# K^T through fp32 words that hold two bf16 values: half as many TensorE transposes in a cached attention decode kernel

## The chip, the cores and the metric

The kernel runs on one core of one Trainium2 chip. The metric is the device time in microseconds (us) of one execution. One chunk below is 2048 cache rows of one head: 1 MB of K and 1 MB of V; there are 256 chunks.

## The reference, cut to what matters

```python
x = A_x                                             # (1, 1, 448)
q = (x @ wq).reshape(1, 1, 16, 256)                 # 16 query heads, 8 KV heads
k = jnp.repeat(k_cache, 2, axis=1)                  # k_cache, v_cache: (1, 8, 65536, 256) bf16
v = jnp.repeat(v_cache, 2, axis=1)
scores = jnp.einsum("bhqd,bhkd->bhqk", q, k) * (256 ** -0.5)
a = jnp.einsum("bhqk,bhkd->bhqd", softmax(scores), v) @ wo     # reshapes cut
# b: a small token-mixing MLP of x, g: a sigmoid gate;  out = g * a + (1 - g) * b
```

The two caches are 537 MB, read once. Everything else is small.

## The kernel before

K and V go through a ring of five 4 MB buffers, one load each for four chunks. TensorE (PE) needs K^T as stationary data for the scores, so every 128x128 block of K is transposed through PSUM. VectorE and ScalarE copy the transposes back to SBUF. Two cuts are marked.

```python
ring = sb([P, NS, DC * NT, DH], bf16, "ring")       # NS = 5 buffers, DC = 4 chunks, NT = 16 tiles, DH = 256
ktT  = sb([P, KTB, NB, 1024], bf16, "ktT")
kst  = psum([P, NB, 1024], bf16, "kst")             # NB = 4 banks
# ... cut ...
def transposes(c):
    # ... waits for the load and for the copies out of kst cut ...
        for j in range(8):
            ntl, dh = divmod(j, 2)
            ins = pe.transpose(kst[:, b, j * P:(j + 1) * P],
                               ring[:, slot, ck * NT + 4 * b + ntl, dh * P:(dh + 1) * P], ident[:, :])
        ins.then_inc(sem_tr, 1)
def scores(c):
    for nt in range(NT):
        b, ntl = divmod(nt, 4)
        for dh in range(2):
            j = 2 * ntl + dh
            ins = pe.matmul(sps[:, c % 2, 2 * nt:2 * nt + 2], ktT[:, slot, b, j * P:(j + 1) * P],
                            qT[:, dh, REP * g:REP * g + REP], start=(dh == 0), stop=(dh == 1))
def values(c):                                       # V is stationary, read with a stride of 2
    # for each of 16 tiles, for dj in 0, 1:
        ins = pe.matmul(acc[:, g % 2, col:col + REP], ring[:, slot, n, dj:DH:2], pT[:, c % PTB, 2 * nt:2 * nt + 2], ...)
for s in range(NC + LAG):                            # NC = 256 chunks
    transposes(s); scores(s - 1); denominators(s - 2); values(s - 2)   # the last 8 chunks' values come at the end
```

Per chunk PE issues 32 transposes, 32 scores matmuls, 1 denominator, 32 values matmuls, each as a weight load and a matmul.

The softmax here doesn't subtract the row's maximum and nothing guards it: scores larger than these inputs give would overflow.

## Time and profile before

| | before |
|---|---|
| time, median of 3 (range) | 1320.84 us (1320.27 to 1323.95) |
| profiled execution | 1318.47 us, span 1316.7 us |
| PE busy, mean granted clock | 86%, 0.765 |
| HBM traffic | 544 MB |

Lines of the page of the kernel before: busy time by engine, granted clock and DMA by slice in tenths, two DMA queues (packets, MB, share of 16 engines' span), and three groups of instructions (count, busy us, mean ns, idle before them).

```profile
PE 1125.9 (86%) x25054; PEld 1098.6 (83%) x25054; DVE 413.8 (31%) x716; ACT 549.1 (42%) x786; POOL 0.9 (0%) x7
...
PEclk9788877787886878777677686677677686887878
DMA  9999999999999999999999999999999999999992
...
q1 hardware_dynamic: 21330, 544.22, 97.1%
q8 instruction: 197, 3.23, 1.0%
...
L261 PE MATMUL kst<-ident,ring 128*128 128x128 bf16 x8192 | 701.3, 263 | 64.3 <-issue 33.0
...
L277 PEld LDWEIGHTS sps<-qT,ktT 128*128 128x128 bf16 x8192 | 248.7, 100 | 53.3 <-issue 52.5
L305 PEld LDWEIGHTS acc<-pT,ring 128*128 128x128 bf16 x8192 | 231.9, 99 | 61.2 <-issue 61.0
```

The DMA row is full but for the tail: the kernel is bound by its data stream. PE is nearly as full, at a clock that moves between full and half. The queue named "instruction" is 197 packets of 16 KB, which are 197 x 256 instructions of 64 bytes, as many as PE executes (2 x 25054 and a few hundred waits). The Trainium skill, "Runtime: NRT & Kernel Launch", section "Instruction fetch mechanics", describes this: an engine's instruction memory is a FIFO that is refilled by DMA in blocks of 16 KiB or 256 instructions. It calls the cost "mostly hidden".

The end of the kernel before: the values of the last eight chunks, then the last projection.

```profile
1304.39 6.04 PE L305 MATMUL acc<-pT,ring 128*128 128x2 bf16 x222
...
1310.88 1.07 PE L305 MATMUL acc<-pT,ring 128*128 128x2 bf16 x34 [0.45 <-issue]
...
1312.70 1.65 PE L317 MATMUL acc<-wo_sb,oTn 128*1 128x448 bf16 x4 [0.76 <-DVE oTn L465]
```

### The profile page before, as it was taken

Reading aid. Unit: us, or ns where it says so; the run is one execution under the profiler, and the core shown is the slowest. Engines: PE = TensorE matmul, PEld = TensorE weight load, DVE = VectorE, ACT = ScalarE, POOL = GpSimd, SP = SyncE. Lnnn points to the kernel's source line nnn. Section 1 sums busy time; section 2 is a strip of 40 time slices with the busy share of each in tenths; the row PEclk is TensorE's granted clock in tenths of the full one; section 3 lists DMA queues with packets and bytes.
Section 4 is the critical chain, followed back from the end, with each engine's and each line's share of the span. In section 5 each row is a group of like instructions: output and inputs, shape, how many; then the busy total and the mean of one; then the engine's idle time right before and its main releaser. Section 6 shows DMA issues by size and latency. Waiting matters only on the chain.

```text
span 1316.7 us, 53063 instructions
## 1 busy us (share of the span) xinstructions
PE 1125.9 (86%) x25054; PEld 1098.6 (83%) x25054; DVE 413.8 (31%) x716; ACT 549.1 (42%) x786; POOL 0.9 (0%) x7
## 2 busy tenths in 40 slices
PE   4888788888889878888888989898888988888887
PEld 4878788888889878888888988888888888888887
DVE  3686232222232322222222222232223232232222
ACT  2444444444444434344334434344444343443433
POOL 0000000000000000000000000000000000000000
PEclk9788877787886878777677686677677686887878
DMA  9999999999999999999999999999999999999992
GB/s 403 430 422 429 430 427 428 424 431 430 430 428 427 426 429 426 426 423 427 424 407 429 429 427 409 418 413 433 426 404 433 414 427 428 426 425 426 418 419 116
DMA packets 21559, 547.62 MB, mean 416 GB/s; under 512 B 2264, under 2 KB 4315, under 8 KB 4702
## 3 DMA queue, kind: packets, MB, share of 16 engines
q1 hardware_dynamic: 21330, 544.22, 97.1%
q8 instruction: 197, 3.23, 1.0%
q14 instruction: 20, 0.16, 0.0%
q10 hardware_dynamic: 12, 0.01, 0.0%
HBM read 544.22 MB, written 0.00 MB: 413 GB/s over the span
## 4 chain that ended last, share of the span: by engine, by line
PE 60%; DMA 31%; issue 8%; DVE 0%; ACT 0%; ACTq 0%; DVEq 0%
PE kst L261 36%; DMA ring<-in_A_k_cache_dram 30%; PE acc L305 11%; PE sps L277 11%; DMA b_b<-in_B_b_dram 1%; PE acc L288 1%; PE acc L317 1%; PE acc L325 0%; PE sps L356 0%; DVE ktT L488 0%; ACT L529 0%; PE sps L358 0%; DVE out_b L479 0%; DVE stat L409 0%; ACTq L521 0%
## 5 line engine op out<-in xcount | busy, mean ns | idle before, releaser
L551 ACT ACTIVATE ktT<-kst 128x1024 bf16<-128x1024 bf16 x512 | 512.0, 1022 | 690.8 <-PE kst L261 690.5
L261 PE MATMUL kst<-ident,ring 128*128 128x128 bf16 x8192 | 701.3, 263 | 64.3 <-issue 33.0
L261 PEld LDWEIGHTS kst<-ident,ring 128*128 128x128 bf16 x8192 | 647.3, 122 | 79.4 <-issue 45.2
L488 DVE COPY ktT<-kst 128x1024 bf16<-128x1024 bf16 x512 | 352.5, 691 | 857.8 <-PE kst L261 844.6
L305 PE MATMUL acc<-pT,ring 128*128 128x2 bf16 x8192 | 252.0, 164 | 56.6 <-issue 56.3
L277 PE MATMUL sps<-qT,ktT 128*128 128x2 bf16 x8192 | 255.5, 164 | 49.7 <-issue 49.3
L277 PEld LDWEIGHTS sps<-qT,ktT 128*128 128x128 bf16 x8192 | 248.7, 100 | 53.3 <-issue 52.5
L305 PEld LDWEIGHTS acc<-pT,ring 128*128 128x128 bf16 x8192 | 231.9, 99 | 61.2 <-issue 61.0
L542 ACT ACTIVATE pT<-sps 128x32 bf16<-128x32 f32 x256 | 50.3, 197 | 48.1 <-PE sps L277 48.0
L288 PE MATMUL acc<-pT,ones_sq 128*128 128x32 bf16 x256 | 45.9, 179 | 0.5 <-ACT pT L542 0.3
L288 PEld LDWEIGHTS acc<-pT,ones_sq 128*128 128x128 bf16 x256 | 25.1, 98 | 0.4 <-ACT pT L542 0.4
L340 PE MATMUL acc<-ones_sq,ktT 1*128 1x1 bf16 x28 | 0.9, 161 | 13.3 <-DMA b_b<-in_B_b_dram 13.3
L340 PEld LDWEIGHTS acc<-ones_sq,ktT 1*128 1x128 bf16 x28 | 0.8, 99 | 13.4 <-DMA b_b<-in_B_b_dram 13.4
L317 PE MATMUL acc<-wo_sb,oTn 128*1 128x448 bf16 x32 | 10.5, 467 | 0.8 <-DVE oTn L465 0.8
L536 ACT ACTIVATE zring<-zring 128x448 bf16<-128x448 bf16 x14 | 8.1, 580 | 0.3 <-issue 0.2
L441 DVE TENSOR_TENSOR zring<-wtmp,uring 128x448 bf16<-128x448 bf16 x14 | 5.5, 392 | 1.5 <-issue 0.5
L439 DVE TENSOR_TENSOR wtmp<-uring 128x448 bf16<-128x448 bf16 x14 | 5.5, 392 | 1.2 <-issue 0.2
L459 DVE TENSOR_TENSOR gu<-wtmp,zring 128x448 bf16<-128x448 bf16 x14 | 5.5, 392 | 1.0
L325 PE MATMUL acc<-gu,w2p_b 128*1 128x448 bf16 x14 | 5.8, 415 | 0.0
L445 DVE TENSOR_TENSOR zring<-uring,wtmp 128x448 bf16<-128x448 bf16 x14 | 5.5, 392 | 1.0
L528 ACT ACTIVATE statb<-statb 1x1 bf16<-1x1 bf16 x1 | 0.2, 206 | 13.2 <-DVE statb L411 13.2
L317 PEld LDWEIGHTS acc<-wo_sb,oTn 128*1 128x1 bf16 x32 | 2.4, 93 | 3.7 <-issue 1.7
(66 smaller groups left out, 63.3 us busy)
## 6 DMA issues: line engine op xcount, KB each, us to landing
ring<-in_A_k_cache_dram SPq DMA_DIRECT2D x64, 4096.0 KB, 29.8
ring<-in_A_v_cache_dram SPq DMA_DIRECT2D x63, 4096.0 KB, 32.3
wo_sb<-in_A_wo_dram SPq DMA_DIRECT2D x8, 448.0 KB, 29.4
ring<-in_A_wq_dram SPq DMA_DIRECT2D x1, 3072.0 KB, 19.3
ring<-in_A_v_cache_dram SPq DMA_DIRECT2D x1, 2048.0 KB, 30.5
ring<-in_A_v_cache_dram SPq DMA_DIRECT2D x1, 1024.0 KB, 32.6
ring<-in_A_v_cache_dram SPq DMA_DIRECT2D x2, 512.0 KB, 33.7
ring<-in_A_wq_dram SPq DMA_DIRECT2D x1, 512.0 KB, 20.1
```

Source lines behind the costliest of these rows:

```text
L261: ins = pe.transpose(kst[:, b, j * P:(j + 1) * P], ring[:, slot, ck * NT + 4 * b + ntl, dh * P:(dh + 1) * P], ident[:, :])
L277: ins = pe.matmul(sps[:, c % 2, 2 * nt:2 * nt + 2], ktT[:, slot, b, j * P:(j + 1) * P], qT[:, dh, REP * g:REP * g + REP], start=(dh == 0), ...
L288: pe.matmul(acc[:, g % 2, DENC:DENC + 2 * NT], ones_sq[:, :], pT[:, c % PTB, :], start=(k == 0), stop=(k == NCPH - 1))
L305: ins = pe.matmul(acc[:, g % 2, col:col + REP], ring[:, slot, n, dj:DH:2], pT[:, c % PTB, 2 * nt:2 * nt + 2], start=False, stop=(k == NCPH ...
L317: ins = pe.matmul(acc[0:1, g % 2, PRC:PRC + DM], oTn[:, g % 2, dj * REP + hh:dj * REP + hh + 1], wo_sb[:, g % 2, hh, dj * DM:(dj + 1) * DM ...
L325: pe.matmul(acc[0:1, 1, PRC:PRC + DM], w2p_b[:, kt:kt + 1], gu[:, kt % NUR, :], start=(kt == 0), stop=(kt == FT - 1)).then_inc(s_bmm, 1)
L439: vec.tensor_tensor(W, U, U, op=ALU.mult)
L441: vec.tensor_tensor(Z, W, U, op=ALU.mult)
L488: vec.tensor_copy(ktT[:, c % KTB, b, :], kst[:, b, :]).then_inc(sem_evd, 1)
L536: act.activation(zring[:, slot, :], zring[:, slot, :], AF.Tanh).then_inc(s_tanh, 1)
L542: act.activation(pT[:, c % PTB, :], sps[:, c % 2, 0:2 * NT], AF.Exp, scale=scale).then_inc(sem_exp, 1)
L551: act.activation(ktT[:, c % KTB, b, :], kst[:, b, :], AF.Copy).then_inc(sem_eva, 1)
```

## The change

The same bytes of K are read as fp32 words, each holding two neighbouring bf16 values, and transposed as such: 16 transposes per chunk instead of 32. The intent is to halve the costliest group on PE. In K^T even and odd columns of the head then alternate, so the scores matmul reads it with a stride of 2, and q is built in even and odd halves to match. The diff, cut to its core:

```diff
+        ring_f = ring.bitcast(f32)
-        ident = sb([P, P], bf16, "ident")
+        ident = sb([P, P], f32, "ident")
-        kst = psum([P, NB, 1024], bf16, "kst")
+        kst = psum([P, NB, 512], f32, "kst")
+        kst_b = kst.bitcast(bf16)
-                    for j in range(8):
-                        ntl, dh = divmod(j, 2)
+                    for j in range(4):
                         ins = pe.transpose(kst[:, b, j * P:(j + 1) * P],
-                                           ring[:, slot, ck * NT + 4 * b + ntl, dh * P:(dh + 1) * P],
-                                           ident[:, :])
+                                           ring_f[:, slot, ck * NT + 4 * b + j, :], ident[:, :])
@@ scores
-                                        ktT[:, slot, b, j * P:(j + 1) * P],
-                                        qT[:, dh, REP * g:REP * g + REP],
+                                        ktT[:, slot, b, ntl * DH + dj:(ntl + 1) * DH:2],
+                                        qT[:, dj, REP * g:REP * g + REP],
@@ cut: the q projection takes every second column of wq; the copies read kst_b, same bytes
```

More of the change, by code (lines that the diff above doesn't have):

```diff
@@ L274, in scores @@
                     b, ntl = divmod(nt, 4)
-                    for dh in range(2):
-                        j = 2 * ntl + dh
+                    for dj in range(2):
                         ins = pe.matmul(sps[:, c % 2, 2 * nt:2 * nt + 2],
-                                        ktT[:, slot, b, j * P:(j + 1) * P],
-                                        qT[:, dh, REP * g:REP * g + REP],
-                                        start=(dh == 0), stop=(dh == 1))
+                                        ktT[:, slot, b, ntl * DH + dj:(ntl + 1) * DH:2],
+                                        qT[:, dj, REP * g:REP * g + REP],
+                                        start=(dj == 0), stop=(dj == 1))
                 ins.then_inc(sem_qk, 1)
@@ L349, in _ @@
                     pe.wait_ge(sem_wq, 32)
-                    for dh in range(2):
+                    for dj in range(2):
                         for h in range(HQ):
-                            j = dh * HQ + h
-                            col = h * DH + dh * P
+                            j = dj * HQ + h
+                            col = h * DH
                             a, cb = divmod(col, HALF)
                             for kt in range(WF):
-                                pe.matmul(sps[:, 1, j:j + 1], wq_a[:, kt, col:col + P], xcol[:, kt:kt + 1],
-                                          start=(kt == 0), stop=False)
-                            ins = pe.matmul(sps[:, 1, j:j + 1], wq_b[:, cb:cb + P],
+                                pe.matmul(sps[:, 1, j:j + 1], wq_a[:, kt, col + dj:col + DH:2],
+                                          xcol[:, kt:kt + 1], start=(kt == 0), stop=False)
+                            ins = pe.matmul(sps[:, 1, j:j + 1], wq_b[:, cb + dj:cb + DH:2],
                                             xcol[:, WF + a:WF + a + 1], start=False, stop=True)
@@ L487, in _ @@
                         vec.wait_ge(sem_tr, NB * c + b + 1)
-                        vec.tensor_copy(ktT[:, c % KTB, b, :], kst[:, b, :]).then_inc(sem_evd, 1)
+                        vec.tensor_copy(ktT[:, c % KTB, b, :], kst_b[:, b, :]).then_inc(sem_evd, 1)
                 if c == 1:
@@ L550, in _ @@
                         act.wait_ge(sem_tr, NB * c + b + 1)
-                        act.activation(ktT[:, c % KTB, b, :], kst[:, b, :], AF.Copy).then_inc(sem_eva, 1)
+                        act.activation(ktT[:, c % KTB, b, :], kst_b[:, b, :], AF.Copy).then_inc(sem_eva, 1)
                 if c >= 1:
```

## The prediction

> **What bounds the kernel now.** The DMA queue. The table of slices shows the 16 DMA engines at 9 tenths in 39 of 40 slices; the stretches from 50 to 1250 us show a DMA share of 1.00 at 420 to 428 GB/s. The queue table gives 544 MB, busy 97.1% of 1316.7 us. The issue list has 30 to 32 us from issue to landing for a 4 MB load, three times the 9.8 us that 4 MB take at 428 GB/s, so two further loads are always queued and the queue never starves. The SyncE waits on PE (746 + 441 us) are for buffers wanted early, not starvation. Per chunk (1 MB of K, 1 MB of V; 256 chunks) the queue needs about 4.95 us.
>
> PE is nearly level with it: busy 86% at a mean granted clock of 0.765. In the timeline 32 transposes take 1.81 us (57 ns each) when the clock is full and 3.44 us (107 ns) when it is halved; the 32 scores matmuls take 0.94 us, the denominator 0.18, the 32 values matmuls 0.94. A chunk is about 3.9 us at full clock, 5.1 to 5.5 at half. PE idles, is throttled, falls behind, catches up: the chain gives it 60% without its being the limit.
>
> **What the change does.** Removes 4096 of 8192 transposes; the other 4096 carry fp32 words. The copies out of PSUM keep their bytes and shapes (ScalarE 1022 ns, VectorE 691 ns). Scores read stationary data with a stride of 2: free, since the values matmuls already do and cost the same as the contiguous scores (weight loads 99 and 100 ns, matmuls 164 and 164). The strided wq reads are 128 matmuls, under 1 us. No HBM bytes change.
>
> **The cost that decides.** The trace has no fp32 matmul. The Trainium skill, "TensorE: Matmul & The Clock Gate", section "Terms", says that transpose mode is 4 times faster for fp32, which I read as one pass instead of four; section "Weight-path perf modes" says that fast weight load is off for fp32, and section "LDWEIGHTS" gives 128 columns at 1.2 GHz, 107 ns. The bf16 side agrees with fast loads: a scores matmul takes 29 ns in all. Estimates for one fp32 transpose from that page: 107 ns if its weight load overlaps the matmul before, 160 ns if not (107 + 53), 214 ns or more if fp32 streams at half rate or in several passes without overlap.
>
> Per chunk: 16 x T + 2.06 us, so 3.8 us at 107 and 4.6 us at 160, both under 4.95, and the DMA still rules. The break-even is about 175 ns. At 214 ns: 5.5 us, about 1440 us in all; at 300 ns about 1780.
>
> **Critical path.** Mid-run nothing can be gained. Only the tail after the last V load (landed about 1302 us; PE then spends 7.5 us on held-back values) depends on PE: at 107 ns perhaps 2 us gained, at 160 ns perhaps 4 lost.
>
> **Predicted:** 1318 us, range 1302 to 1500. Faster by over 2%: 0.03; within 2%: 0.60; slower: 0.37.
>
> **What would show it.** Right: DMA still 9 tenths throughout, 97% share, transposes 100 to 170 ns apart, scores group unchanged, PE busy no higher than about 90%. Wrong: transposes over 175 ns apart, PE and not DMA full in the slices, granted clock near 1.0 in spite of it, GB/s down, SyncE waiting longer for the K transposes.
>
> **What would make it wrong.** fp32 transposes that stream at a lower rate, take several passes, or load their own weights without overlap; a stride of 2 that slows weight loads of the copied K; a different granted clock. A gain over 2% would need a DMA rate above anything the slices show.

## More of the kernel before

PE's waits in the kernel before (total us, times, longest us). "issue" means that the profile shows nothing that the engine waited for.

```profile
PE acc L305 <- issue: 56.3, 52, 2.6
PE sps L277 <- issue: 49.3, 39, 2.7
PE kst L261 <- issue: 33.0, 27, 2.9
PE kst L261 <- DMA ring<-in_A_k_cache_dram: 29.7, 23, 3.3
```

PE stands still for 139 us (the first three lines) for nothing that the profile shows, in holes of up to 2.9 us in the midst of a run of equal matmuls, and waits for K for only 30 us. One such hole in the timeline of the kernel before (start us, duration us; idle before it in brackets):

```profile
799.85 0.49 PE L277 MATMUL sps<-qT,ktT 128*128 128x2 bf16 x14
802.28 0.44 PE L277 MATMUL sps<-qT,ktT 128*128 128x2 bf16 x12 [1.95 <-issue]
802.58 0.18 PE L288 MATMUL acc<-pT,ones_sq 128*128 128x32 bf16 x1
```

Weight loads of two chunks in the timeline of the kernel before, the first with the clock full, the second with it halved (a window on it shows PEclk 0.50):

```profile
1258.19 1.79 PEld L261 LDWEIGHTS kst<-ident,ring 128*128 128x128 bf16 x32
1259.94 0.91 PEld L277 LDWEIGHTS sps<-qT,ktT 128*128 128x128 bf16 x32
...
1261.60 0.46 PEld L261 LDWEIGHTS kst<-ident,ring 128*128 128x128 bf16 x8
...
1272.71 3.33 PEld L261 LDWEIGHTS kst<-ident,ring 128*128 128x128 bf16 x32 [1.91 <-DMA ring<-in_A_k_cache_dram]
1276.00 1.06 PEld L277 LDWEIGHTS sps<-qT,ktT 128*128 128x128 bf16 x32
...
1277.86 0.24 PEld L261 LDWEIGHTS kst<-ident,ring 128*128 128x128 bf16 x3
```

From one start to the next: 32 transposes take 1259.94 - 1258.19 = 1.75 us (55 ns each) at full clock and 3.29 us (103 ns) at half; a whole chunk takes 3.41 us and 5.15 us.

## The result, and the profile after

| | before | after |
|---|---|---|
| time, median of 4 (range) | 1321.59 us (1320.27 to 1323.95) | 1308.71 us (1308.40 to 1309.20) |
| profiled span | 1316.7 us | 1306.8 us |
| PE instruction blocks of 16 KB | 197 | 165 |
| PE idle for "issue" | 139 us | 13 us |
| PE idle for the K loads | 30 us | 195 us |

The ratio is 0.9901, with a 95% interval of 0.9884 to 0.9918: same by the 2% rule, but clearly 1% faster. All ratios here are the mean time of one kernel's runs over that of the other's runs of the same rounds, so they are not quite the ratio of the medians quoted. The output is correct.

The same lines of the page of the kernel after:

```profile
PE 1075.7 (82%) x20958; PEld 1050.5 (80%) x20958; DVE 413.8 (32%) x716; ACT 541.1 (41%) x786; POOL 0.9 (0%) x7
...
PEclk9777887867878678878778786886887877878878
DMA  9999999999999999999999999999999999999993
...
q1 hardware_dynamic: 21330, 544.22, 97.7%
q8 instruction: 165, 2.70, 0.8%
...
L262 PE MATMUL kst<-ident,ring 128*128 128x128 f32 x4096 | 663.8, 331 | 198.6 <-DMA ring<-in_A_k_cache_dram 194.9
...
L276 PEld LDWEIGHTS sps<-qT,ktT 128*128 128x128 bf16 x8192 | 253.0, 99 | 13.6 <-issue 5.4
...
L304 PEld LDWEIGHTS acc<-pT,ring 128*128 128x128 bf16 x8192 | 226.3, 98 | 9.0 <-issue 8.7
```

The stride of 2 costs nothing (weight loads of the scores 99 ns against 100). The transposes halved in number, but their busy time fell only from 701 to 664 us, and the clock, which was halved for 536 us instead of 621, can account for part of that. PE's waits after:

```profile
PE kst L262 <- DMA ring<-in_A_k_cache_dram: 194.9, 60, 5.5
...
PE acc L304 <- issue: 7.8, 12, 1.4
PE sps L276 <- issue: 4.4, 8, 1.8
...
PE kst L262 <- issue: 1.0, 3, 0.4
```

What PE used to lose to "issue" it now spends waiting for data, which is where an engine that is not the bottleneck should wait. Weight loads of two chunks after, the first at half clock, the second at full:

```profile
1247.13 3.27 PEld L262 LDWEIGHTS kst<-ident,ring 128*128 128x128 f32 x16 [5.16 <-DMA ring<-in_A_k_cache_dram]
1250.39 1.12 PEld L276 LDWEIGHTS sps<-qT,ktT 128*128 128x128 bf16 x32
...
1252.27 1.74 PEld L262 LDWEIGHTS kst<-ident,ring 128*128 128x128 f32 x16
1253.98 0.96 PEld L276 LDWEIGHTS sps<-qT,ktT 128*128 128x128 bf16 x32
...
1255.69 0.42 PEld L262 LDWEIGHTS kst<-ident,ring 128*128 128x128 f32 x4
```

Sixteen fp32 transposes take 1.71 us at full clock (107 ns each) and 3.26 us at half (204 ns). One fp32 transpose costs what two bf16 ones cost (2 x 55 and 2 x 103). A whole chunk takes 3.42 us at full clock, against 3.41 before; over all chunks that ran at full clock with no pause of PE, the medians are 3.414 us (91 chunks) and 3.415 us (38 before). The chunk that began at half clock took 5.14 us, against 5.15 before, but the full clock came back before its end; of only two chunks after the change that ran wholly at half clock without a pause, the shorter took 5.23 us. **The fp32 form makes PE's work no shorter; the gain is not there.** The end of the kernel after:

```profile
1294.21 2.58 PE L304 MATMUL acc<-pT,ring 128*128 128x2 bf16 x94
...
1297.52 4.54 PE L304 MATMUL acc<-pT,ring 128*128 128x2 bf16 x162 [0.73 <-issue]
...
1302.82 1.65 PE L316 MATMUL acc<-wo_sb,oTn 128*1 128x448 bf16 x4 [0.76 <-DVE oTn L464]
```

Where the 9.9 us between the two profiled spans lie follows from the trace's record of every DMA packet (start, duration, queue). This table is computed from those records ("data" is K, V and weights; the last packets are those of the last 0.5 MB of V; the stretches are counted in bins of 50 ns, and other bins move their number by one or two):

```
                                                      before    after
first to last data packet                             1301.0   1295.1 us
last data packet to the end of the span                 13.9      9.9 us
data packets, sum over 16 engines / 16                1278.7   1276.6 us
instruction packets, sum / 16                           12.9     10.9 us
engines short of 16 packets in flight, / 16             13.9     12.1 us
mid-run stretches >= 0.5 us with < 14.5 in flight    9 (13.3)  9 (6.4 us)
PE idle over 0.4 us, times, of any cause / of these
  ending 1.2 to 1.7 us after a block landed          129 / 107   78 / 19
blocks, from one landing to the next: 10% / median  6.1 / 6.4   6.1 / 7.2 us
```

Six us come out of the stream and four out of the tail. In the stream, instruction packets, idle engines and the data packets themselves give about 2 us each; why data packets are 0.2% shorter was not tested. So a late PE would account for about 6 of the 9.9 us (the tail and the idle engines), the traffic of the instruction blocks for 2, and 2 stay open. The block row is the key: while the DMA is full, blocks of 256 PE instructions hardly ever land nearer than 6 us to each other. A chunk before needed 194 instructions, 0.76 of a block or 4.6 us at that pace, close to its 4.95 us of DMA time; after, 162 instructions or 3.9 us. Before, 107 of the 129 idle stretches end 1.2 to 1.7 us after a block lands, a window that covers only 7.5% of the time.

**Theory A:** the gain comes from the shorter instruction stream. Blocks late for PE made it late in freeing ring buffers, so the DMA ran short now and then, and made holes in the tail, where PE is all that is left. **Theory B:** the gain comes from less array work, the cheaper transposes. A third suspect is the granted clock, which rose from 0.765 to 0.796.

### The profile page after: what moved, and what is told of

It is laid out like the page before. It is cut to its first block, busy times and chain, and to the rows that moved or that the text cites. A ratio compares the mean times of both kernels' runs of the same rounds, so it can differ in the third digit from the quotient of the medians. Undisturbed runs are those within 1.5% of the kernel's fastest.

```text
span 1306.8 us, 44871 instructions
## 1 busy us (share of the span) xinstructions
PE 1075.7 (82%) x20958; PEld 1050.5 (80%) x20958; DVE 413.8 (32%) x716; ACT 541.1 (41%) x786; POOL 0.9 (0%) x7
## 3 DMA queue, kind: packets, MB, share of 16 engines
q1 hardware_dynamic: 21330, 544.22, 97.7%
## 4 chain that ended last, share of the span: by engine, by line
DMA 71%; PE 26%; DVE 1%; issue 1%; ACT 0%; DVEq 0%; ACTq 0%
DMA ring<-in_A_k_cache_dram 70%; PE kst L262 17%; PE acc L304 4%; PE sps L276 4%; DMA b_b<-in_B_b_dram 1%; PE acc L287 0%; DVE ktT L487 0%; ACT zring L535 0%; PE sps L355 0%; PE acc L316 0%; DVE zring L440 0%; DVE gu L458 0%; DVE zring L444 0%; DVE wtmp L438 0%; DVE wtmp L434 0%
## 5 line engine op out<-in xcount | busy, mean ns | idle before, releaser
L262 PE MATMUL kst<-ident,ring 128*128 128x128 f32 x4096 | 663.8, 331 | 198.6 <-DMA ring<-in_A_k_cache_dram 194.9
L262 PEld LDWEIGHTS kst<-ident,ring 128*128 128x128 f32 x4096 | 594.7, 174 | 211.1 <-DMA ring<-in_A_k_cache_dram 203.3
L276 PEld LDWEIGHTS sps<-qT,ktT 128*128 128x128 bf16 x8192 | 253.0, 99 | 13.6 <-issue 5.4
L276 PE MATMUL sps<-qT,ktT 128*128 128x2 bf16 x8192 | 248.4, 164 | 5.5 <-issue 4.4
L304 PE MATMUL acc<-pT,ring 128*128 128x2 bf16 x8192 | 243.6, 163 | 7.9 <-issue 7.8
L304 PEld LDWEIGHTS acc<-pT,ring 128*128 128x128 bf16 x8192 | 226.3, 98 | 9.0 <-issue 8.7
L434 DVE TENSOR_SCALAR wtmp<-hbT,params 128x448 bf16<-128x448 bf16 x14 | 4.7, 336 | 1.3
```

The source lines that it names most:

```text
L262: ins = pe.transpose(kst[:, b, j * P:(j + 1) * P], ring_f[:, slot, ck * NT + 4 * b + j, :], ident[:, :])
```

## The experiments

All twelve gave the answer that the output test accepts. That means little for those that are wrong: the softmax here is so flat that the test can't tell. Kernels are compared only within the same rounds.

### pad2 and pad4: empty instructions after the change (void)

```diff
@@ after, transposes, behind each pe.transpose
+                        for _ in range(2):        # pad4: range(4)
+                            pe.nop(nofuse=True)
```

> The kernel after, with two empty instructions on TensorE behind each fp32 transpose: 8192 more instructions, as many as the change removed, and no array work. Theory A (the gain comes from the shorter instruction stream: its 16 KB blocks land at best about 6 us apart while the data saturates the DMA, and PE stalls for them): 197 instruction blocks again instead of 165, idle 'issue' gaps of PE back from 13 us to over 100 us, time back at 1317 to 1324 us. Theory B (the gain comes from cheaper transposes, 109 ns instead of 2 x 57 ns): 1307 to 1311 us, as after.

> The same with four empty instructions per transpose: 229 blocks. Theory A: 229 blocks at 6.1 us cannot be had in less than 1397 us, so the instruction stream is the bound: 1395 to 1430 us, DMA visibly short of full. Theory B: empty instructions cost nothing of the array: 1307 to 1312 us. If instead the empty instructions cost issue time by themselves, PE would show it without the blocks being evenly spaced at about 6 us.

Measured: 1308.47 us (ratio 0.9889) and 1308.52 us (0.9889). Neither theory is touched: the traces show 165 blocks in both, so the empty instructions had been removed when the program was built, and both runs are repeats of the kernel after. Their use is as a measure of it: 1307.9 to 1309.0 us, with 24 to 27 us of PE holes instead of 13.

### b_few_instr: bf16 transposes kept, fewer instructions

```diff
@@ before, scores
-                    for dh in range(2):
-                        j = 2 * ntl + dh
-                        ins = pe.matmul(sps[:, c % 2, 2 * nt:2 * nt + 2], ktT[..., j * P:(j + 1) * P],
-                                        qT[:, dh, ...], start=(dh == 0), stop=(dh == 1))
+                    j = 2 * ntl
+                    ins = pe.matmul(sps[:, c % 2, 2 * nt:2 * nt + 128].rearrange("p (a r) -> p a r", r=REP),
+                                    ktT[..., j * P:(j + 1) * P],
+                                    qT[:, 0:1, ...].broadcast_to((P, 64, REP)), start=True, stop=True)
```

> The kernel before, bf16 transposes kept, but the scores of a chunk made by 16 matmuls 128 columns wide instead of 32 matmuls 2 wide (half the contraction: wrong result on purpose). Array time about the same (16 x 57 = 0.91 us against 0.94), 8192 fewer instructions. Theory A: 165 blocks, gaps of PE mostly gone, 1306 to 1312 us although no transpose is cheaper. Theory B: 1318 to 1324 us, as before.

Measured: 1307.81 us (1306.39 to 1309.39), ratio 0.9884 (0.9857 to 0.9912), with 165 blocks. PE's waits in this run:

```profile
PE kst L261 <- DMA ring<-in_A_k_cache_dram: 220.4, 62, 5.7
...
PE acc L304 <- issue: 8.1, 10, 1.5
```

With every bf16 transpose still in place, the time is that of the kernel after, and so is the pattern of waits. Array work did not shrink: a chunk at full clock without a pause takes 3.54 us here, against 3.41 before. Theory B falls. One caution: the wide matmuls also changed the clock (0.885 on average, 302 us at half clock against 621 before). The next run takes that apart.

### b_half_rows: all instructions kept, less array work

```diff
@@ before, transposes
-                        ins = pe.transpose(kst[:, b, j * P:(j + 1) * P],
-                                           ring[:, slot, ...], ident[:, :])
+                        ins = pe.transpose(kst[:, b, j * P:j * P + 64],
+                                           ring[0:64, slot, ...], ident[0:64, 0:64])
```

(kst is zeroed once at the start.)

> The kernel before with each transpose cut to 64 rows and 64 columns (wrong result on purpose): the same instructions, but the array work of a transpose about halved (57 to about 30 ns), over 100 us less in all, far more than the fp32 form saves. Theory B: at least as fast as after, 1300 to 1309 us. Theory A: 197 blocks at 6.1 us are 1202 us, so PE would keep up mid-run, but the tail still waits for its blocks and the instruction traffic stays: 1312 to 1319 us.

Measured: 1320.09 us (1316.76 to 1325.21), ratio 0.9978 (0.9946 to 1.001): the same as before, a microsecond above the range given to theory A and far from that of theory B. The waits, and two groups of weight loads in the timeline of this run:

```profile
PE acc L305 <- issue: 100.9, 61, 2.9
PE sps L277 <- issue: 78.1, 55, 2.5
...
PE kst L261 <- issue: 55.3, 46, 2.6
```

```profile
606.74 1.73 PEld L261 LDWEIGHTS kst<-ident,ring 64*128 64x128 bf16 x32 [0.41 <-DMA ring<-in_A_k_cache_dram]
608.55 0.69 PEld L277 LDWEIGHTS sps<-qT,ktT 128*128 128x128 bf16 x23
```

The premise was wrong: 64 rows are no cheaper (32 in 608.55 - 606.74 = 1.81 us, 57 ns each). But something else changed. The clock line of this run reads 1.000, with no half-clock time at all, so PE's busy time fell all the same, from 1126 to 987.5 us. That makes the run a better test than planned: a full clock and 138 us less busy time, with the long instruction stream kept, are worth about 2 us, which the interval does not tell from none. PE turned what it saved into holes, 234 us instead of 139. Neither array time nor the clock is what held the kernel before. (Theory A had expected PE to keep up mid-run; it did not.)

### a_dup and b_dup: each transpose issued as two of 64 rows

```diff
@@ after (a_dup; b_dup is the same edit in before)
+                        for h in range(2):
+                            ins = pe.transpose(kst[:, b, j * P + 64 * h:j * P + 64 * h + 64],
+                                               ring_f[0:64, slot, ck * NT + 4 * b + j, :], ident[0:64, 0:64])
```

> The kernel after with each fp32 transpose issued as two of 64 rows and 64 columns (the same rows twice: wrong result on purpose). 8192 instructions more, 197 blocks as before; the array time of a pair should be that of one full transpose, about 110 ns, which the timeline will tell. This is what the empty instructions of the first call were to do; they had been taken out when the program was compiled (their run had 165 blocks), so that run said nothing. Theory A (instruction stream): 'issue' gaps of PE over 100 us again, 1316 to 1323 us. Theory B (cheaper transposes): 1307 to 1311 us if a pair costs up to 120 ns.

> The kernel before with each bf16 transpose issued as two of 64 rows (wrong result on purpose): 16384 instructions more, 261 blocks, array time about as before. Theory A: if a block cannot land oftener than every 6 us, 261 of them take 1570 us, and the kernel takes 1500 to 1620 us with the DMA short of full; if the 6 us come only from standing behind data on full DMA engines, they shrink as the DMA drains, and it is 1350 to 1500 us. Theory B: 1318 to 1330 us.

Measured: 1439.86 us (ratio 1.0883) and 1580.44 us (1.1926). Against before or after neither is a test of A: as in the run before, a transpose of 64 rows costs as much as one of 128, so the array work of the transposes doubled. The transposes of one chunk of a_dup:

```profile
602.49 3.67 PE L263 MATMUL kst<-ident,ring 64*128 64x64 f32 x32
```

A chunk of a_dup (from one group of transposes to the next) takes 607.92 - 602.49 = 5.43 us, and 256 of them are 1390 us: it is bound by PE, which is 99% busy with almost no holes. That 64 rows are no cheaper agrees with the Trainium skill, "TensorE: Matmul & The Clock Gate", section "LDWEIGHTS", by which a weight load costs its columns and not its rows. In a_dup the fp32 transposes pass 64 moving columns instead of 128 and still go at about 113 ns, so their rate is that of their weight load. The prediction's budget of PE time agrees in its sum: it put transposes of 214 ns at 5.5 us a chunk and about 1440 us in all. Its parts were off in opposite directions: the pairs took 3.61 us of a chunk and the rest 1.83, against 16 x 214 ns = 3.42 and 2.06.

Compared with each other, the two runs are the cleanest test of A. Their array work per chunk is nearly equal (5.43 us in a_dup and 5.35 in b_dup for a chunk without a pause; PE busy 1416.8 and 1420.5 us), both ran at a granted clock of 1.000, and in neither did PE wait more than 2 us for K. What differs much is the number of instructions: 197 blocks against 261. b_dup takes 140.6 us longer, and its holes are 137.5 us against 0.3. PE's waits in b_dup:

```profile
PE kst L262 <- issue: 67.1, 68, 2.1
PE sps L278 <- issue: 34.8, 40, 2.0
PE acc L306 <- issue: 33.0, 35, 2.1
```

Of its 127 holes over 0.4 us, 125 end 1.2 to 1.7 us after a block landed. Here PE is the limit, so the holes show in full in the time; the pair does not tell how much of them shows where the DMA is the limit. Sorted by how many DMA engines were busy meanwhile, the times between its blocks are:

```
b_dup, engines busy   blocks   least    median
under 12                58     3.30     3.80 us
over 15.5              123     4.96     6.63 us
```

So the 6 us are not the fetch alone: with the DMA half drained a block comes in under 4 us.

### a_few_instr: still fewer instructions after the change

The edit of b_few_instr, made in the kernel after (wrong).

> The kernel after with the scores in 16 matmuls of 128 columns (wrong result on purpose): another 8192 instructions fewer, 133 blocks. Theory A: the gaps are already nearly gone after, so only the rest of them in the tail (about 1 us) and a sixth of the instruction traffic (2 of 11 us of DMA time) are left to gain: 1303 to 1308 us. Theory B: 1307 to 1311 us.

Measured: 1300.72 us (1300.26 to 1301.78), ratio 0.9831 (0.9805 to 0.9858). It has 133 blocks, under 1 us of PE holes, and takes 8 us less than the kernel after. That is more than either theory was given, though on A's side. The packet records put 6.5 us in the stream (first to last data packet 1288.6 us) and 1.7 in the tail; instruction packets take 2.1 us less and data packets again 3 us less. As in b_few_instr, the clock rose too (0.874); a_more_wide below, at 0.882 with 169 blocks, gained nothing from such a clock. So a shorter instruction stream goes on paying after the holes are gone, and why the data packets shorten with it stays open.

### a_more_small and a_more_wide: the instructions put back

```diff
@@ after, scores (a_more_small)
                 for nt in range(NT):
+                    pe.matmul(sps[:, c % 2, 64:64 + REP], ktT[:, slot, 0, 0:P],
+                              qT[:, 0, REP * g:REP * g + REP], start=True, stop=True)
@@ after, scores (a_more_wide), before the loop
+                for _ in range(2):
+                    pe.matmul(sps[:, c % 2, :], ones_sq[:, :], ktT[:, slot, 0, 0:512], start=True, stop=True)
```

> The kernel after with 16 more 2-column matmuls per chunk into unused PSUM columns (correct result): 8192 more instructions, 197 blocks as before the change, and about 16 x 27 = 0.43 us of array time per chunk, 111 us in all, which the 195 us that PE waited for K can take. Theory A: gaps of PE over 80 us again, 1316 to 1324 us. Theory B (only array time counts): the same time as the run with 2 wide matmuls, 1308 to 1313 us.

> Its control: the kernel after with 2 more 512-column matmuls per chunk (correct result): the same array time (2 x 216 ns = 0.43 us per chunk) in 1024 more instructions, 169 blocks. Theory A: few gaps, 1309 to 1314 us, of which about 3 us for eight chunks of the tail at 0.43 us each. Theory B: equal to the run with 16 small ones.

Measured: 1330.08 us (1318.86 to 1335.22), ratio 1.0042 (1.0002 to 1.0083), with 197 blocks and 77 us of holes, and 1311.17 us (1308.95 to 1311.97), ratio 0.9912 (0.9891 to 0.9934), with 169 blocks and 22 us of holes. Putting the 8192 instructions back as small matmuls takes away the whole gain and more; the median lies 6 us above the range that theory A was given. The same nominal array time in few instructions costs 2.5 us. That is theory A's side again, though the holes stayed just under the 80 us expected, and the control is not clean: at a mean clock of 0.766 against 0.882 the small version also spent twice as long at half clock (626 against 312 us) and PE had no slack left (it waited 1.9 us for K). How much of the 19 us between the two is the clock can't be read from this pair.

### b_8k: smaller data packets

```diff
@@ before, load(): every K and V load in four DMAs of 16 tiles (the counts waited for are adapted)
+                    for k in range(DC):
+                        eng.dma_start(ring[:, slot, k * NT:(k + 1) * NT, :]..., cache_src(w, cd, k * NT, (k + 1) * NT)
+                                      ).then_inc(sem_in[slot], 16)
```

> The kernel before with every K and V load in four DMAs of 1 MB, so that a data packet is 8 KB (309 ns in the traces) instead of 32 KB (1214 ns); correct. If an instruction block takes 6 us because it stands behind about four data packets, 4 x 309 + 1050 ns is 2.3 us: blocks as near as 2.3 to 3 us, 'issue' gaps of PE under 20 us instead of 139. The 8 KB packets move 424 GB/s instead of 432, so the stream takes 1.8% or 23 us more and the kernel 1325 to 1345 us all the same. If the 6 us are the instruction fetch's own, the gaps stay over 100 us and the time is over 1340 us.

Measured: 1342.51 us (1342.25 to 1343.10), ratio 1.0152 (1.0126 to 1.0178). The idea behind this run started from the Trainium skill, "DMA: Bandwidth & Descriptors", section "Queues, rings and completion order": each engine goes round robin between queues at packet granularity, and a packet there is a group of typically 9 to 17 descriptors, which need not be what the trace counts as a packet. That a block stands behind about four of the trace's data packets was the expectation's own estimate. It falls: while the DMA was full, the blocks came no nearer (5.8 us at least, median 6.4), although the data packets were a quarter as long. The time is near the upper end of what the slower packets alone were expected to cost. The holes shrank to 70 us, between the two expectations; with data packets using 1318.5 us of engine time instead of 1278.7, each chunk leaves PE more time, so this says little.

### a_kpieces and a_tail8k: a shorter tail

```diff
@@ after (a_kpieces): the last K load but one in four pieces with a semaphore each
+                if (w, cd) == ("k", NCD - 2):
+                    for k in range(DC):
+                        eng.dma_start(ring[:, slot, k * NT:(k + 1) * NT, :]..., ...).then_inc(sem_kp[k], 16)
+                    return
@@ transposes
+                if cd == NCD - 2:
+                    pe.wait_ge(sem_kp[ck], 16)
@@ a_tail8k: also the last five loads, in four DMAs each on the buffer's own semaphore
```

> The kernel after, with the last K load but one in four pieces of 1 MB, each with its own semaphore, so that PE can start the last eight chunks when the first MB has landed. The tail after the last data is 12.4 us of PE work, and PE idles about 4 us before it for the whole 4 MB and restarts at half clock: 1302 to 1306 us, correct. If it is no faster, the end is not set by PE's start of these chunks.

> The kernel after with the last K load but one in four pieces, as in the run before, and the last five loads in 8 KB packets too, so that the 4 us of PE gaps in the tail should go, for under 1 us of DMA time; correct. 1300 to 1304 us, faster than both kernels; if the gaps in the tail stay, 1306 to 1308 us.

Measured: 1306.91 us (1306.15 to 1307.90), ratio 0.9878, and 1306.51 us (1305.84 to 1307.38), ratio 0.9879, both correct. The first missed its range by a us, the second by 2.5, and landed where it had been expected if the holes in the tail stay. (The tail of 12.4 us in the first expectation leaves out the last 1 MB of V, which comes in smaller packets; counted from the last data packet it is 9.9 us.) In a_kpieces PE reached the final values 2.3 us earlier than in the kernel after and lost it there:

```profile
1291.90 2.51 PE L312 MATMUL acc<-pT,ring 128*128 128x2 bf16 x92
1296.82 4.57 PE L312 MATMUL acc<-pT,ring 128*128 128x2 bf16 x164 [2.41 <-issue]
```

A hole of 2.41 us stands where the kernel after has one of 0.73: PE arrived sooner at an instruction block that came when it came (it landed at 1295.48 us, and at 1296.00 in the kernel after). With smaller data packets in the tail, a_tail8k still has holes of 0.93 and 0.20 us there. All 12 runs of the two are below all runs of the kernel after and its two repeats, but by about 2 us; their ratios to before overlap with its own. They were run at other times. They are at best about 0.15% faster.

## Why the prediction was right or wrong

**Right: the range, and what bounds the kernel.** The DMA row stays full, the queue share is 97.7%, and the time is within 2% and within 1302 to 1500 us. That the range held is in part luck: the prediction foresaw a gain of 2 or 3 us, and no reasoning of its own leads to a time 9 us below its 1318.

**Right: the cost of an fp32 transpose.** Of the three estimates from "TensorE: Matmul & The Clock Gate" the first holds at full clock: 107 ns with the weight load overlapped, measured 107. a_dup supports the reason, that the weight load sets the rate. The prediction did not say that this too doubles at half clock (204 ns), nor draw the conclusion that the timeline allows at once: two bf16 transposes are 110 ns, so the change takes nothing off PE. The stride of 2 was free, as said.

**Mis-sized: "Mid-run nothing can be gained" and the tail ("at 107 ns perhaps 2 us gained").** The medians are 12.9 us apart, against 3 predicted. In the profiled pair the tail gave 4.0 us and the stream 5.9. The missing term is the instruction stream. The change removed 8192 of some 50,000 PE instructions, and the prediction counted only their array time. For the tail, too, the cheaper transposes that it counted on are not the reason, since a chunk takes as long as before.

**Wrong: why PE was late before.** "PE idles, is throttled, falls behind, catches up" left out the 139 us of "issue" holes, which the view of waits had shown from the start, next to an instruction queue of 197 packets. b_half_rows never throttled at all and gained 2 us; it kept the holes.

**Wrong in a small way: "the queue never starves".** A median of 30 us from issue to landing hides the exceptions: nine stretches, 13.3 us in all, with engines short of work. They stand where a late PE freed a buffer late: all nine begin within 2 us of the issue of a K load that had waited for PE's values, as at 819.4, 841.1 and 862.4 us (issues at 819.3, 840.9 and 862.4). Two loads were still on their way each time. But the 16 completions of a load come in two groups of eight, 17.7 and 29.3 us after its issue in the median, and at 820 us the group that is ahead was finishing the last load that it had: 11 of 16 packets were in flight. The landing is that of the last engine, and the prediction took it for all sixteen.

Shown: array time and the granted clock do not explain the gain (the chunk times are equal, and b_half_rows), and the time follows the number of instructions with either kind of transpose (b_few_instr, a_few_instr, a_more_small, and b_dup against a_dup). Only argued: the split of the stream's 6 us into its three parts, and the share of the clock in a_more_small. Open: what sets the 6 us between blocks while the DMA is full. A quarter of the data packet's size left it as it was; in b_dup it fell where the DMA was half drained.

## What to carry to other kernels

On a kernel that keeps the DMA full, count TensorE's instructions as well as its array time: in this one 256 of them could be had about every 6 us, and matmuls of 26 ns with their weight loads (the 32 of the scores take 0.84 us at full clock) use them up in 3.4 us. Holes marked "issue" in a run of equal matmuls, ending shortly after an instruction packet lands, are the sign. When a change halves a count and leaves the array time alone, look for the gain there, and fuse small matmuls before splitting them.

## What the Trainium skill lacked or had wrong

- "Runtime: NRT & Kernel Launch", section "Instruction fetch mechanics", calls crossing a 16 KiB block "mostly hidden". With the DMA engines full it was not: 139 us of PE holes in 1316.7 us, 107 of the 129 over 0.4 us ending 1.2 to 1.7 us after a block landed, and blocks 6.1 us apart at the 10% point (3.3 us at least when the engines drained in b_dup). The page gives no rate for the fetch under DMA load.
- "DMA: Bandwidth & Descriptors" has round robin at packet granularity, but does not say how long an instruction block waits among data. With data packets of 8 KB instead of 32 KB in the trace, the median from block to block stayed at 6.4 us.
- "TensorE: Matmul & The Clock Gate", section "LDWEIGHTS", divides columns by 1.2 without saying how that moves with the clock. fp32 transposes, bound by that load, took 107 ns at full clock and 204 ns at half. The 4-fold gain of fp32 in transpose mode ("Terms") did not make one fp32 transpose cheaper than two bf16 ones (2 x 55 ns).
- The same page, "PE-mode transpose", says that the full clock does not engage for transposes. Here, in a stream that holds other matmuls too, runs of 32 bf16 transposes went at 55 ns, and at 103 ns when the clock was halved.
- No page says why kernels with transposes of 64 rows were never throttled (clock 1.000 at 75% busy in b_half_rows, and at 99% in a_dup) while the same ones of 128 rows were at 0.765, or why a bf16 transpose of 64 rows and columns still took 57 ns, when the scores' weight loads of as many columns followed each other in 26 ns.
